# A Fourier mix and sliding-window attention kernel: x's second block loaded early, ring rows, pads and column tiles made by other engines, splits on GpSimd until the masks begin, and a re-ordered tail

## The chip, the core and the metric

The kernel runs on one core of a Trainium2 chip. The metric is the device time of one execution in microseconds (us). Matrix products run on TensorE (PE), elementwise work on VectorE (DVE), ScalarE (ACT) and GpSimd (POOL); SyncE (SP) issues nearly all DMA transfers, in the order of its queue.

## The reference

x has 2048 rows of 512. Two branches are computed from it and mixed row by row with a sigmoid gate:

```
g = sigmoid((x * gate_w).sum(-1))
a, b = x @ dft_hid_re.T, x @ dft_hid_im.T
A = dft_seq_re @ a - dft_seq_im @ b              # Fourier mix, real part
q, k, v = split(x @ wqkv)                        # 32 heads of 16
p = softmax(mask(q k^T / 4))                     # causal, window of 256 keys
B = (p v) @ wo
out = g * A + (1 - g) * B
```

Everything is float32. The kernel splits each float32 operand of the large products into a high part in fp32r and a low remainder, and multiplies three of the four combinations (`TERMS`).

## The kernel before, in words

TensorE's order is written out by the program. One loop over steps n, with four pairs p in each, issues the scores of step n (`s_pair`, L363), the transposed scores of step k = n - 19 (`t_pair`, L445), every few steps the products with v (`pv`, L471), and between them matmuls drawn by `fill` from a generator, `dense`, which holds all other matrix work: v and qk projections (L300 "dv", L277 "dqk"), the hidden transforms ("dab"), and the sequence transform in blocks of 48 matmuls ("dc", L523). The other engines' orders are laid out by a scheduler, with some instructions pinned behind a marked one (`behind`, `mark`, `late`).

What the change touches:

- **Start.** x comes as four blocks of 512 rows, each 512 x 512 values in two loads (`load_x`, L127). Block 0 goes into "pt" buffers, the later ones into the two "raw" buffers, which hold wv first. `split_x` (L133) makes the high part (L78 on ScalarE, L80 on VectorE) and the low part (L81, VectorE). Block 1's casts are made by ScalarE, those of blocks 2 and 3 by VectorE, all as jobs that run between the v projections.
- **Weights.** `split_soon` (L105) queues a cast and a subtraction for each half of a 128 x 1024 weight; `job` runs one of them at every third of six matmuls. All are on VectorE, at the line of `late` (L579).
- **Rings and pads.** "ring" holds q and k in a layout of 128 rows, of which rows 96 to 128 are cleared by GpSimd (L199). A pad (`make_pad`, L333) is the stationary operand of a score; its rows 96 to 128 are set once, for the first kind by GpSimd from x's first low part (L203), for the second by GpSimd memsets and VectorE products (L211, L214). The column tiles "half", "side" and "mrow" are made by GpSimd selects.
- **Evictions.** A qk or ab product is split from PSUM by ScalarE and VectorE into one of three "home" tiles (L84, L86, L88) and stored by SP.
- **Row sums.** Every eight steps `ml_split` (VectorE), `ml_turn` (two small matmuls, L383) and `ml_rows` (VectorE) bring row maxima and sums into the other layout, at places given by `TURN`.
- **v.** `v_load` brings v rows ("vr", one buffer); `v_spread` (L428, GpSimd) spreads them into "vpad". From step 19 on GpSimd also masks the transposed scores (L450, L454).
- **Tail.** After the loop `attention_done` loads and splits wo into the space of ring0. For each block of 128 rows (token block), `wo_prep` loads o and splits it, and `wo_block` multiplies it with wo (12 matmuls, L793) and adds the result to what the other branch left (L795). Between the last dc blocks these are issued in two batches of 96 matmuls.

Of the kernel before, what the change touches and what calls it, by code (L numbers as in the profile page):

```python
# [14 lines left out]
P = 128  # L15
# [17 lines left out]
def fnet_window_mix(ctx: ExitStack, tc: tile.TileContext, xT, x, wqk, wv, wr, wi, cr, ci, wo, gw, out):  # L33
# [40 lines left out]


    def split(hi, lo, raw, act=False):
        if act:
            nc.scalar.copy(hi, raw)  # L78
        else:
            nc.vector.tensor_copy(hi, raw)  # L80
        nc.vector.tensor_sub(lo, raw, f(hi))  # L81

# [44 lines left out]
    def load_x(ss, j):  # L127
        raw = st.tile([P, 1024], F32, name="raw", bufs=2)
        ld(raw.rearrange("p (k s) -> p k s", k=2), xT[ss, 2 * j:2 * j + 2].rearrange("k p s -> p k s"))
        for c in range(2):  # L130
            XRAW[2 * j + c, ss] = raw[:, HALVES[c]]

    def split_x(ss, dks, act=False):  # L133
        for dk in dks:
            XT[dk, ss] = big.tile([P, 2, 512], F32R, name="big")
            split(XT[dk, ss][:, 0], XT[dk, ss][:, 1], XRAW.pop((dk, ss)), act)

# [30 lines left out]
    for h in (0, 64):  # L168
# [6 lines left out]
    nc.gpsimd.memset(f(ident[:]), 1.0)  # L175
    nc.gpsimd.affine_select(ident[:], f(ident[:]), pattern=[[1, P]], compare_op=OP.is_equal, fill=0.0,
                            base=0, channel_multiplier=-1)

    cols = const.tile([P, 4], F32, name="half")
    half, side = cols[:, :2], cols[:, 2:]  # L180
    mrow = const.tile([P, 2], F32, name="mrow")
    for t, edges in ((half, ((0, 16, 32, 48, 64, 80), (16, 32, 48, 64, 80, 96))), (mrow, ((96, 98), (98, 100)))):
        nc.gpsimd.memset(t, 0.0)
        for h in range(2):
            for i, e in enumerate(edges[h]):
                a = t[:, h:h + 1]
                nc.gpsimd.affine_select(a, a, pattern=[[0, 1]], compare_op=OP.is_ge, fill=1.0 - i % 2,
                                        base=e - 1, channel_multiplier=-1)

    nc.vector.reduce_sum(side[:, 0:1], f(ident[:]).rearrange("p (r h) -> p h r", h=2)[:, 0],  # L190
                         axis=mybir.AxisListType.X)
    nc.vector.tensor_scalar(side[:, 1:2], side[:, 0:1], -1.0, 1.0, op0=OP.mult, op1=OP.add)

# [3 lines left out]
    def clear_rows(i, ss):  # L197
        with behind("pool"):
            nc.gpsimd.memset(f(ring[i][96:128, :, ss * 512:(ss + 1) * 512]), 0.0)  # L199

    first_lo = f(XT[0, 0][96:128, 1]).rearrange("r (p c) -> r p c", p=NP)
    for t in pads[0]:
        mark("pool", nc.gpsimd.affine_select(t[96:128], first_lo, pattern=[[0, NP], [0, P]], compare_op=OP.is_gt,  # L203
                                             fill=0.0, base=0, channel_multiplier=0))
    clear_rows(1, 0)
    clear_rows(0, 0)
    vpad = [const.tile([P, 4, NP, 32], F32, name=f"vpad{b}") for b in range(2)]

    def clear_pads():
        for t in pads[1]:  # L210
            nc.gpsimd.memset(f(t[96:128]), 1.0)  # L211
            for h in range(2):
                a = turned(t)[96:128, :, :, h]
                nc.vector.tensor_scalar(a, f(a), mrow[96:128, h:h + 1], None, op0=OP.mult)  # L214


# [117 lines left out]
    def make_pad(i, n):  # L334
# [3 lines left out]
        b = n % NB  # L338
        with behind(*(("act", "dve") if n < NPAD else ())):
            for h in range(2):  # L340
                src = f(ring[i][:96, :, b * BQ:(b + 1) * BQ])
                dst = turned(t)[:96, :, :, h] if i else t[:96, :, 64 * h:64 * h + 64]
                if i and h:
                    nc.scalar.activation(dst, src, AF.Copy, scale=half[:96, h:h + 1])  # L344
                else:
                    nc.vector.tensor_scalar(dst, src, half[:96, h:h + 1], None, op0=OP.mult)  # L346
# [190 lines left out]

    def c_final(get, ab, r):
        ps = ps_d.tile([P, 512], F32, name="dc", tag="d")
        g = g1[:, 15:16]  # L540
        for j in range(2):
            w = get((1, 30 + j))
            yield from c_part(w, range(16)[8 * j:8 * j + 8 - 2 * j], ab, ps, (0, 13))
            yield
        late(nc.vector.scalar_tensor_tensor, r, ps, g, r, OP.mult, OP.add)
        for c, dma in ((slice(0, 256), nc.sync), (slice(256, 512), nc.scalar)):
# [39 lines left out]
    def dense():  # L586
        warm()
        with behind("sp"):
            wraw = [load_raw(wv[i]) for i in range(2)]
        wvs = [late(split_raw, r, True) for r in wraw]  # L590
        qk_first(wq0)
        load_x(1, 0)
        load_x(1, 1)
        yield
        def x_job(ss, dk):
            late(split_x, ss, (dk,), ss == 1)
            if dk % 2 and ss < 3:
                load_x(ss + 1, dk // 2)

# [121 lines left out]
        ab = nxt  # L721
        wait = []

        mixed = {}

# [19 lines left out]
        for tb in range(SWITCH, 16):  # L745
            if FIN:
                while ended:
                    ended.pop(0)()
            if tb in O:
                mixed[tb] = wo_block(tb, 0)  # L750
            for w in [w for w in wait if w in O]:
                wait.remove(w)
                ld(out[w], wo_block(w, 1))
            if FIN and tb < 15:
                for w in (tb + 1, *wait[:-(-len(wait) // (15 - tb))]):
                    wo_prep(w)
            yield from c_block(pieces.get, 1, tb, ab, add_r) if tb < 15 else c_final(pieces.get, ab, mixed.pop(15))

    FIN = []

    def attention_done():
# [70 lines left out]
    ring_ahead(0)  # L832
    need(("v", 5))

# [9 lines left out]
    for n in range(N + LAG + 1):  # L844
        if n in (1, 3, 5):
            for i in range(2):
                clear_rows(1 - i, (n + 1) // 2)
        if n == 7:
            clear_pads()
        k = n - LAG  # L850
        ring_ahead(n + 1)
        if k in (-1, 4):
# [5 lines left out]
        for p in range(NP):  # L858
# [9 lines left out]
            fill(n)  # L868
            for at_n, at_p, do in TURN:
                u, j = divmod(n - at_n, 8)  # L870
# [64 lines left out]
```

## Time and profile before

| | us |
|---|---|
| runs before | 852.27, 853.18, 858.51 (median 853.18) |
| the profiled execution's own time | 854.57 |
| its span, from the first to the last instruction | 852.9 |
| TensorE busy | 844.8 |
| VectorE busy | 615.8 |
| ScalarE busy | 593.7 |
| GpSimd busy | 251.9 |

The profile is of one execution on hardware. A line of a group names the source line, engine, operation, output and inputs, count, busy time and mean duration. A timeline row gives start, duration, engine, line, operation, and in brackets the idle time before it and what ended it. PEld is TensorE's weight load, SPq SyncE's queue.

### The profile page before, as it was taken

Reading aid. Unit: us, or ns where it says so; the run is one execution under the profiler, and the core shown is the slowest. Engines: PE = TensorE matmul, PEld = TensorE weight load, DVE = VectorE, ACT = ScalarE, POOL = GpSimd, SP = SyncE. Lnnn points to the kernel's source line nnn. Section 1 sums busy time; section 2 is a strip of 40 time slices with the busy share of each in tenths; the row PEclk is TensorE's granted clock in tenths of the full one; section 3 lists DMA queues with packets and bytes.
Section 4 is the critical chain, followed back from the end, with each engine's and each line's share of the span. In section 5 each row is a group of like instructions: output and inputs, shape, how many; then the busy total and the mean of one; then the engine's idle time right before and its main releaser. Section 6 shows DMA issues by size and latency. Waiting matters only on the chain.

```text
span 852.9 us, 16687 instructions
## 1 busy us (share of the span) xinstructions
PE 844.8 (99%) x5166; PEld 691.3 (81%) x5166; DVE 615.8 (72%) x2013; ACT 593.7 (70%) x1793; POOL 251.9 (30%) x585
## 2 busy tenths in 40 slices
PE   9999999999999999999999999999999999999998
PEld 7788788788788888888878887888888887877887
DVE  5588978667878787669777787788888774437531
ACT  5388798878888987779878897778777765532200
POOL 9000222333332333333423324333243354510000
PEclk9999999999999999999999999999999999999999
DMA  7876578576675275444435557989784344359542
GB/s 255 276 235 201 172 247 249 198 236 210 205 249 181 59 210 127 152 125 143 148 120 145 164 144 216 286 278 292 242 225 140 117 153 144 124 176 303 158 147 98
DMA packets 94344, 160.99 MB, mean 189 GB/s; under 512 B 26800, under 2 KB 35760, under 8 KB 94256
## 3 DMA queue, kind: packets, MB, share of 16 engines
q1 hardware_dynamic: 93824, 159.28, 59.8%
q8 instruction: 40, 0.66, 0.3%
q10 hardware_dynamic: 432, 0.66, 0.2%
q14 instruction: 48, 0.39, 0.1%
HBM read 108.27 MB, written 51.64 MB: 187 GB/s over the span
## 4 chain that ended last, share of the span: by engine, by line
PE 92%; DMA 4%; DVE 2%; ACT 1%; issue 1%; SPq 0%; DVEq 0%; ACTq 0%
PE dc L523 39%; PE dab L300 10%; PE s L363 9%; PE t L445 8%; PE o L471 8%; PE dqk L277 8%; PE t L793 5%; PE dv L300 4%; DMA raw<-xT 1%; DMA fin<-o_scr 1%; DMA o_scr<-ev 1%; DVE sm L365 1%; DMA pt<-wqk 0%; DVE big L81 0%; SPq L56 0%
## 5 line engine op out<-in xcount | busy, mean ns | idle before, releaser
L368 ACT ACTIVATE sm<-sm,ml 128x320 f32<-128x320 f32 (+4 forms) x512 | 277.9, 544 | 101.1 <-DVE ml L365 96.4
L523 PE MATMUL dc<-big,hi 128*128 128x512 f32 x1020 | 344.4, 393 | 0.0
L365 DVE CUSTOM_DVE_ANT_0 sm<-s,mask 128x320 f32<-128x320 f32 (+4 forms) x512 | 235.3, 464 | 113.2 <-PE s L363 91.5
L523 PE MATMUL dc<-big,lo 128*128 128x512 f32 x510 | 200.6, 393 | 0.0
L523 PEld LDWEIGHTS dc<-big,hi 128*128 128x128 f32 x1020 | 179.7, 188 | 21.4
L446 ACT ACTIVATE pt<-t 128x320 f32<-128x320 f32 (+4 forms) x392 | 160.3, 411 | 43.0 <-PE t L445 40.9
L450 POOL TENSOR_SCALAR_AFFINE_SELECT pt<-pt 128x128 f32<-128x128 f32 x196 | 72.2, 368 | 302.0 <-ACT pt L446 299.8
L363 PE MATMUL s<-ring,pad 128*128 128x320 f32 (+4 forms) x512 | 157.7, 308 | 0.0
L445 PE MATMUL t<-ring,pad 128*128 128x320 f32 (+4 forms) x512 | 154.1, 301 | 0.1
L346 DVE TENSOR_SCALAR pad<-ring,half 96x256 fp32r<-96x256 f32 x384 | 119.9, 358 | 13.5 <-PE t L445 13.3
L363 PEld LDWEIGHTS s<-ring,pad 128*128 128x128 f32 x512 | 96.1, 188 | 30.3 <-issue 9.0
L445 PEld LDWEIGHTS t<-ring,pad 128*128 128x128 f32 x512 | 96.1, 188 | 22.0 <-DVE ml L365 1.0
L523 PEld LDWEIGHTS dc<-big,lo 128*128 128x128 f32 x510 | 95.9, 188 | 13.8 <-issue 1.6
L368 ACT ACTIVATION_READ_ACCUMULATOR sm<-sm,ml 128x1 f32 x512 | 97.7, 191 | 0.0
L428 POOL TENSOR_SCALAR vpad<-vr,half 128x256 f32<-128x256 f32 x64 | 60.5, 958 | 124.9 <-DMA vr<-v_scr 75.7
L579 DVE TENSOR_TENSOR lo<-raw,hi 128x512 fp32r<-128x512 f32 x142 | 96.8, 691 | 0.1
L300 PE MATMUL dab<-hi,big 128*128 128x512 f32 x256 | 89.2, 394 | 0.0
L277 PE MATMUL dqk<-big,hi 128*128 128x512 f32 x240 | 85.7, 394 | 1.5 <-DVE big L81 0.9
L579 DVE CAST hi<-raw 128x512 fp32r<-128x512 f32 x142 | 60.1, 432 | 18.7 <-PE dc L523 13.0
L344 ACT ACTIVATE pad<-ring,half 96x256 fp32r<-96x256 f32 x128 | 66.6, 520 | 0.0
L454 POOL TENSOR_SCALAR_AFFINE_SELECT pt<-pt 128x128 f32<-128x128 f32 x172 | 62.0, 361 | 0.1
L446 ACT ACTIVATE home<-t 128x320 f32<-128x320 f32 (+4 forms) x120 | 49.0, 408 | 13.4 <-PE t L445 11.5
(97 smaller groups left out, 915.3 us busy)
## 6 DMA issues: line engine op xcount, KB each, us to landing
qk_scr<-home SPq DMA_DIRECT2D x32, 512.0 KB
ring<-qk_scr SPq DMA_DIRECT2D x32, 512.0 KB
raw<-cr SPq DMA_DIRECT2D x32, 512.0 KB
raw<-ci SPq DMA_DIRECT2D x32, 512.0 KB
r_scr<-ev SPq DMA_DIRECT2D x42, 256.0 KB
ev<-r_scr SPq DMA_DIRECT2D x42, 256.0 KB
ab_scr<-home SPq DMA_DIRECT2D x20, 512.0 KB
big<-ab_scr SPq DMA_DIRECT2D x20, 512.0 KB
```

Of the source, the lines that this page charges most:

```text
L277: nc.tensor.matmul(ps, w[a][:, c:c + 128], XT[dk, ss][:, b], start=n == 0, stop=n == 11)
L300: nc.tensor.matmul(ps, XT[dk, ss][:, a, c * 128:(c + 1) * 128], wh[b], start=n == 0, stop=n == 11)
L346: nc.vector.tensor_scalar(dst, src, half[:96, h:h + 1], None, op0=OP.mult)
L363: nc.tensor.matmul(ps[:, :w], PAD[0, n][:, p], ring[1][:, p, k0:k0 + w], start=True, stop=True)
L365: mark("dve", nc.vector.tensor_tensor_reduce(out=sm[:, :w], in0=ps[:, :w], in1=mask[:, WIN - w:], scale=1.0, scalar=3e38, op0=OP.add, op1= ...
L368: mark("act", nc.scalar.activation(sm[:, :w], sm[:, :w], AF.Exp, bias=nm[:, c], scale=-1.0, accum_out=l[:, c]))
L445: nc.tensor.matmul(ps[:, :w], PAD[1, n][:, p], ring[0][:, p, q0:q0 + w], start=True, stop=True)
L446: nc.scalar.activation(pt[:, p, :w], ps[:, :w], AF.Exp, scale=-1.0)
L450: nc.gpsimd.affine_select(a, a, pattern=[[0, 2], [2, 64]], compare_op=OP.is_ge, fill=0.0, base=1, channel_multiplier=-1)
L471: nc.tensor.matmul(OT[g, sb][32 * p:32 * p + 32, q - sb * 512:e - sb * 512], v2[:, p], pt[:, p, q - q0:e - q0], start=first, stop=kb == 8 ...
L523: nc.tensor.matmul(ps, w[a][:, i % 8 * 128:i % 8 * 128 + 128], ab[SC[i]][:, b], start=i == ends[0] and a + b == 0, stop=i == ends[1] and a ...
L579: return fn(*args)
```

## The change

It does nine things. Block 1 of x goes into "pt" buffers and is loaded right behind wv, and block 2 then goes into "raw" where block 1 went. Ring rows are cleared in one go, behind a select that reads x's first high part instead of two that read its low part. The second pad of the first kind and the pads of the second kind get their rows from ScalarE. The column tiles are made by VectorE reductions of the identity. Block 3's casts are made by GpSimd, its subtractions stay on VectorE. Weight splits are made by GpSimd until `masks` is filled, at step 19. Pads of the first kind are pinned behind VectorE's last marked instruction up to step 24. The first turn of the row sums is issued at (10, 0) and (10, 1) instead of (9, 1) and (9, 2). In the tail a new `tail_step` runs ahead of every 12 dc matmuls: it multiplies up to two token blocks that were prepared more than two ticks ago, and prepares others, at most seven at a time.

```diff
 def split(hi, lo, raw, act=False):
     if act:
         nc.scalar.copy(hi, raw)
     else:
-        nc.vector.tensor_copy(hi, raw)
-    nc.vector.tensor_sub(lo, raw, f(hi))
+        cast = (nc.gpsimd if act is None else nc.vector).tensor_copy(hi, raw)
+        if act is None:
+            mark("pool", cast)
+    return nc.vector.tensor_sub(lo, raw, f(hi))
...
 # split_soon
-    jobs.append(lambda c=c: late(nc.vector.tensor_copy, hi[:, c], raw[:, c]))
-    jobs.append(lambda c=c: late(nc.vector.tensor_sub, lo[:, c], raw[:, c], f(hi[:, c])))
+    jobs.append(lambda c=c: late((nc.vector if masks else nc.gpsimd).tensor_copy, hi[:, c], raw[:, c]))
+    jobs.append(lambda c=c: late((nc.vector if masks else nc.gpsimd).tensor_sub, lo[:, c], raw[:, c], f(hi[:, c])))
...
 # load_x, split_x
-    raw = st.tile([P, 1024], F32, name="raw", bufs=2)
+    raw = pt_raw() if ss == 1 else st.tile([P, 1024], F32, name="raw", bufs=2)
...
+    for t, run in ((half, 16), (side, 1)):
+        nc.vector.reduce_sum(t[:, 0:1], f(ident[:]).rearrange("p (g h x) -> p h g x", h=2, x=run)[:, 0],
+                             axis=mybir.AxisListType.XY)
...
+first_hi = f(XT[0, 0][96:128, 0]).rearrange("r (p c) -> r p c", p=NP)
+mark("pool", nc.gpsimd.affine_select(pads[0][0][96:128], first_hi, ...))
+for ss in range(4):
+    for i in (1, 0):
+        clear_rows(i, ss)
...
 # clear_pads
+    nc.scalar.activation(pads[0][1][96:128].rearrange("r p c -> r (p c)"),
+                         f(XT[0, 0][96:128, 0]), AF.Copy, scale=0.0)
     for t in pads[1]:
-        nc.gpsimd.memset(f(t[96:128]), 1.0)
         for h in range(2):
-            nc.vector.tensor_scalar(a, f(a), mrow[96:128, h:h + 1], None, op0=OP.mult)
+            nc.scalar.activation(turned(t)[96:128, :, :, h], mask[96:128, :256]...,
+                                 AF.Identity, bias=mrow[96:128, h:h + 1], scale=0.0)
...
 # dense
     with behind("sp"):
         wraw = [load_raw(wv[i]) for i in range(2)]
+        load_x(1, 0)
+        load_x(1, 1)
     wvs = [late(split_raw, r, True) for r in wraw]
     qk_first(wq0)
-    load_x(1, 0)
-    load_x(1, 1)
+    load_x(2, 0)
+    load_x(2, 1)
     def x_job(ss, dk):
-        late(split_x, ss, (dk,), ss == 1)
-        if dk % 2 and ss < 3:
-            load_x(ss + 1, dk // 2)
+        late(split_x, ss, (dk,), ss == 1 or (None if ss == 3 else False))
+        if dk % 2 and ss == 2:
+            load_x(3, dk // 2)
...
 # c_part
     for i in chunks:
+        if FIN and i % 4 == 0:
+            tail_step()
...
+def tail_step():
+    t = next(clock)
+    for tb in [tb for tb in O if born[tb] < t - 2][:2]:
+        if tb in wait:
+            wait.remove(tb)
+            ld(out[tb], wo_block(tb, 1))
+        else:
+            mixed[tb] = wo_block(tb, 0)
+    for tb in (*wait[:5], 15, 14, *wait[5:]):
+        if tb not in O and tb not in mixed and len(O) < 7 and (tb > now[-1] or tb in wait):
+            wo_prep(tb)
+            born[tb] = t
...
+FIRST = (8, 1, ml_split), (10, 0, ml_turn), (10, 1, ml_rows), (12, 0, m_ring)
...
+    if k == 0:
+        masks.append(n)
...
-        for at_n, at_p, do in TURN:
+        for at_n, at_p, do in TURN if n > 12 else FIRST:
```

More of the change, by code (lines that the diff above doesn't have):

```diff
@@ L338, in make_pad @@
         b = n % NB
-        with behind(*(("act", "dve") if n < NPAD else ())):
+        with behind(*(("act", "dve") if n < NPAD else ("dve",) if i == 0 and n < 24 else ())):
             for h in range(2):
@@ L745, in dense @@
         for tb in range(SWITCH, 16):
-            if FIN:
+            now.append(tb)
+            if tb == 15:
                 while ended:
                     ended.pop(0)()
-            if tb in O:
-                mixed[tb] = wo_block(tb, 0)
[L751 to L759, printed above, removed]
+            yield from c_block(pieces.get, 1, tb, ab, add_r) if tb < 15 else c_final(pieces.get, ab)
+    FIN = []
+    now = []
+    wait = []
+    mixed = {}
+    born = {}
+    clock = iter(range(99))
+    def tail_step():
[5 more added lines that the diff above has]
+            else:
+                mixed[tb] = wo_block(tb, 0)
+        for tb in (*wait[:5], 15, 14, *wait[5:]):
+            if tb not in O and tb not in mixed and len(O) < 7 and (tb > now[-1] or tb in wait):
+                wo_prep(tb)
+                born[tb] = t
     def attention_done():
```

55 lines of the change are left out of this document (23 added, 32 removed).

## The prediction, made before the changed kernel had run

> **What bounds the kernel now.** I read the page first, then who TensorE waited for, then its timeline around each wait, then the engine named there.
>
> ```profile
> span 852.9 us, 16687 instructions
> PE 844.8 (99%) x5166; PEld 691.3 (81%) x5166; DVE 615.8 (72%) x2013; ACT 593.7 (70%) x1793; POOL 251.9 (30%) x585
> ...
> PEclk9999999999999999999999999999999999999999
> ```
>
> TensorE is busy 99% at an undisturbed clock, and the change neither adds nor takes away a matmul. So nothing can be won except the moments in which TensorE stands still, and these can be listed.
>
> ```profile
> PE dqk L277 <- DVE big L81: 0.9, 1, 0.9
> ...
> PE t L793 <- ACT os L78: 0.6, 1, 0.6
> ```
>
> Columns: total us, times, longest. Three more waits of this kind stand below with their releaser. The ends of matmuls are modelled, so I measure a stall from start to start. The unhindered pace comes from the chain in order of time (start, us, what), the stalls from TensorE's timeline (start, us, ..., idle time before).
>
> ```profile
> 11.46 3.57 DMA raw<-xT
> ...
> 29.52 5.67 PE dv L300 x25
> ...
> 783.33 22.54 PE t L793 x96
> ```
>
> ```profile
> 8.07 0.73 PE L265 MATMUL s<-big,hi 128*128 128x512 f32 x2 [0.37 <-DVE big L81]
> ...
> 24.76 0.39 PE L277 MATMUL dqk<-big,hi 128*128 128x512 f32 x1
> 26.05 0.50 PE L277 MATMUL dqk<-big,hi 128*128 128x512 f32 x1 [0.91 <-DVE big L81]
> ...
> 94.15 0.27 PE L383 MATMUL s<-ident,mlh 128*64 128x128 f32 x1 [0.72 <-DVE mlh L377]
> ...
> 99.92 0.50 PE L277 MATMUL dqk<-big,hi 128*128 128x512 f32 x1 [0.64 <-DVE home L86]
> ...
> 102.93 0.63 PE L277 MATMUL dqk<-big,hi 128*128 128x512 f32 x2
> 103.68 0.41 PE L445 MATMUL t<-ring,pad 128*128 128x320 f32 x1
> ...
> 783.33 6.97 PE L793 MATMUL t<-fin,os 128*128 128x512 f32 x28 [0.59 <-ACT os L78]
> ```
>
> A 512-column matmul starts every 5.67 / 25 = 0.227 us and is shown as 0.39 long; so a shown idle time is about 0.16 short. At 26: 26.05 - 24.76 - 0.23 = 1.06. In the same way 0.37 + 0.16 = 0.53 at 8.07, 0.88 at 94, 0.80 at 99.9 and 0.75 at 783.33; the 96 matmuls behind this last took 22.54 where 96 x 0.227 = 21.8, so 0.75 more. At 103.68 it is 103.68 - 102.93 - 0.45 = 0.30. In all 5.07, that is 0.6% of the run, and the most this change can take, beside some 0.1 us with which the pipeline restarts behind a stall (0.3 to 0.4 in all).
>
> **The change part by part.** *x's second block.* It goes into two pt buffers and is issued right behind wv, before the third block, on the same SP queue.
>
> ```profile
> 6.94 1.07 DVE L81 TENSOR_TENSOR big<-pt,big 128x512 fp32r<-128x512 f32 x1 [1.08 <-ACT big L78]
> ...
> 8.28 0.68 DVE L81 TENSOR_TENSOR big<-pt,big 128x512 fp32r<-128x512 f32 x1
> ...
> 23.73 0.43 DVE L80 CAST big<-raw 128x512 fp32r<-128x512 f32 x1 [4.42 <-DMA raw<-xT]
> ...
> 25.31 0.69 DVE L81 TENSOR_TENSOR big<-raw,big 128x512 fp32r<-128x512 f32 x1
> ```
>
> ```profile
> 17.48 0.59 ACT L311 COPY ev<-dv 128x512 f32<-128x512 f32 x1 [0.80 <-PE dv L300]
> ```
>
> The wait at 26.05 is not for the second block's load. VectorE stands until 23.73 for block three, whose cast is queued ahead of the last subtraction of block two (25.31, ends 26.0). In the changed order the four subtractions of block two stand together, ahead of block three. ScalarE's casts for them come later, since five pad instructions of at most 512 columns follow the copy at 17.48, at most 0.6 each: 3 us, then a cast, a copy and a cast, 1.8. The last cast ends near 22.9 and the last subtraction near 23.6, against 24.8 when TensorE wants it. So 1.06 plus a restart of 0.1 go: **1.15**. If the early load held wv back, TensorE would wait at its first dv matmul instead, at most the 3.57 us that this load took from issue to landing (11.46 to 15.03); but wv is issued ahead of it, and as many bytes stand behind wv as before. Bounds: -2.4 to 1.2; I take the upper end, since the rows name the cast of block three as the releaser's holder and none names wv.
>
> *Ring clearing and pads.* POOL now has one select behind x's first high part instead of two behind the low one; the column tiles become three more reduces on VectorE near 3 us, and two products behind x's splits, some 0.2 us each, far from anything that TensorE wants.
>
> ```profile
> 6.25 1.23 POOL L203 TENSOR_SCALAR_AFFINE_SELECT pad<-big 32x512 fp32r<-32x512 f32 x2
> 7.42 14.09 POOL L199 MEMSET ring<- 32x2048 f32 x8
> ...
> 90.97 1.84 POOL L428 TENSOR_SCALAR vpad<-vr,half 128x256 f32<-128x256 f32 x2 [67.98 <-DMA vr<-v_scr]
> 100.54 2.38 POOL L428 TENSOR_SCALAR vpad<-vr,half 128x256 f32<-128x256 f32 x2 [7.72 <-DMA vr<-v_scr]
> ```
>
> The subtraction at 6.94 took 1.07 while POOL's selects ran (6.25 to 7.48); its twin at 8.28 took 0.68 while POOL only cleared the ring. It is the releaser of the wait at 8.07. With the selects gone from there it should end 0.39 earlier: **0.4**. The remaining select moves to 4.85, beside the first subtraction; its result is wanted at 5.94, and 0.4 later it is still just in time. Bounds: -0.2 to 0.5. The Trainium skill, "SBUF — State Buffer", Who interferes with whom, says that a VectorE instruction with two SBUF inputs contends with a GpSimd instruction that reads SBUF, not with one that only writes; the two rows agree.
>
> *Splits by POOL.* Until the masks begin (step 19, 100.9 us), 4 casts of x's last block and 5 casts with 5 subtractions of weights leave VectorE, and 4 pad products go to ScalarE.
>
> ```profile
> 91.19 0.80 DVE L579 TENSOR_TENSOR lo<-raw,hi 128x512 fp32r<-128x512 f32 x1
> ...
> 92.02 0.48 DVE L365 CUSTOM_DVE_ANT_0 sm<-s,mask 128x320 f32<-128x320 f32 x1
> ...
> 93.88 0.21 DVE L377 TENSOR_TENSOR mlh<-ml,mlh 128x64 fp32r<-128x64 f32 x1
> ...
> 97.21 0.61 DVE L346 TENSOR_SCALAR pad<-ring,half 96x256 fp32r<-96x256 f32 x2
> ...
> 99.18 0.69 DVE L86 TENSOR_TENSOR home<-dqk,home 128x512 fp32r<-128x512 f32 x1
> ...
> 100.60 1.01 DVE L346 TENSOR_SCALAR pad<-ring,half 96x256 fp32r<-96x256 f32 x2
> ```
>
> The waits at 94, 99.9 and 103.7 are all for VectorE late in its own queue: in this stretch its operations follow each other without a gap, and of what stands ahead of the eviction at 99.18, three casts and two subtractions (by the rows above 3 x 0.43 + 2 x 0.69 = 2.7 us) are weight splits that now go to POOL. The eviction was 0.8 late, so it has room. The first transposition's result at 93.88 has 0.43 + 0.80 + 0.43 = 1.6 fewer us ahead of it and was 0.9 late. Here 2.0 us of stalls (0.88 + 0.80 + 0.30) with two restarts should go; I take **1.9**, since VectorE has little slack there. The turn itself is moved only for the first eight steps, at 66.5 us, where TensorE did not wait: nothing.
>
> What POOL needs for a 128x512 cast or subtraction, no row shows. From below: 8 memsets of 2048 columns in 14.09, so 0.44 for 512. The select reads and writes 512 columns in 0.62. From above: vpad's products, 256 columns in 0.92, give 1.85 for a cast, and twice that, 3.7, for two inputs. I take 0.7 and 1.2, near the select, whose plain run of 512 columns is most alike.
>
> ```profile
> 68.70 0.69 PE dv L300 x3
> ...
> 81.94 0.68 PE dqk L277 x3
> ```
>
> By the chain, TensorE leaves the first qk weight, and with it a buffer, near 68.7, where it goes over to dv, and wants the next weight near 81.9. 2 x 0.7 + 2 x 1.2 = 3.8 us split it by 72.5, 11.1 us at the upper price by 79.8. So POOL's idle time hides it at either end; without that cover VectorE would do it, as before.
>
> *The tail.* The wo blocks, formerly two batches of 96 matmuls, come two at a time between 12 dc matmuls, early token blocks first.
>
> ```profile
> 771.21 6.50 DMA o_scr<-ev
> 777.73 4.90 DMA fin<-o_scr
> ```
>
> ```profile
> 773.63 0.62 ACT L78 CAST os<-fin 128x512 fp32r<-128x512 f32 x1 [0.16 <-DMA fin<-o_scr]
> ...
> 782.66 0.62 ACT L78 CAST os<-fin 128x512 fp32r<-128x512 f32 x1 [6.25 <-DMA fin<-o_scr]
> ```
>
> ```profile
> 777.49 0.68 DVE L81 TENSOR_TENSOR fin<-raw,fin 128x512 fp32r<-128x512 f32 x1
> ```
>
> The wait at 783.33 is for the last o_scr block (stored at 771, landed 777.7, loaded back by 782.6). Now the first blocks are token blocks 0 to 3, whose casts ended by 774.3. They begin 24 matmuls (5.4 us) earlier, at 777.4; the last wo weight is subtracted by 778.2 and wanted at 779.2 to 779.7. Token blocks 15 and 14 are wanted at 796 and 802. VectorE's first sum waits behind their subtractions (784.6); with four PSUM buffers TensorE needs that sum only at 793.8. So 0.75 + 0.75 go, less what the interleaving may cost at first: **1.1**; bounds -1.5 (if the last wo weight is 2.6 us late) to 1.5.
>
> **Sum.** 1.15 + 0.4 + 1.9 + 1.1 = 4.55: the profiled execution's span of 852.9 becomes 848.3, and its time of 854.57 becomes 850.0. It lies 1.4 above the median of the runs, 853.18; from the median I forecast **848.6**. With all stalls and restarts gone (5.4) and the runs' lower edge of 852.27 it is 846.9.
>
> **The rivals.** *One: VectorE gains little, since POOL gets in its way.* For it speaks that the two pads at 100.60 took 1.01 beside POOL's vpad and the two at 97.21 took 0.61, and the subtraction at 91.19 0.80 instead of 0.69. If each of ten POOL operations costs VectorE 0.4, 4 of the 5.6 us taken off it (5 x 0.43 + 5 x 0.69) come back, and of the 1.9 about 0.4 stays: 853.18 - (1.15 + 0.4 + 0.4 + 1.1) = 850.1. Against it: the s operation at 92.02, of the kind that fills VectorE, took 0.48 beside vpad, no more than others. The same section of the Trainium skill calls the shared port an exclusive lock held for the whole instruction; by that a clash with a POOL subtraction of 1.2 costs up to 1.2, and rival one would hold.
>
> *Two, slower: SyncE stands behind POOL.* In the changed queue the second vr load, which waits for POOL's vpad, comes ahead of the store of the next qk eviction, and vpad comes behind POOL's weight splits.
>
> ```profile
> 90.27 4.81 SPq L56 DMA_DIRECT2D qk_scr<-home  x2
> ...
> 97.09 0.37 SPq L56 DMA_DIRECT2D vr<-v_scr  x1
> ```
>
> Buffers two and three come free near 81.9, behind the last dv matmul, and three casts and three subtractions follow: at the upper price 81.9 + 3 x 5.55 + 1.84 = 100.4 for vpad, and the store due at 95 goes out 5 us late; the third vr load repeats it with the next (vr lands 3.4 later, vpad takes 2.4: 106.2 instead of 98, an estimate from 95 and a turn of 3.3). Three home tiles at 3.3 us a turn give 10 us; 8 late and 3 to land misses that, ScalarE stands in an eviction with the exponentials behind it, and TensorE follows by some 3 us each time. 6 lost and 1.9 not won: 853.18 - 2.65 + 6 = 856.5. It decides from a cast and a subtraction that take 4.45 together (then vpad ends after 97.1). Against it: the select's 0.62.
>
> *Three: the tail's wait only moves.* A ci load now goes ahead of three o loads, and a ci cast stands between the two last subtractions of wo. If it lands 2.6 us late, the tail loses 1.5 instead of winning 1.1: 851.2.
>
> **How the numbers follow.** Forecast 0.70, rival one 0.13, two 0.10, three 0.05, more than 1% faster 0.02 (no row shows that much idle time). The range reaches from 846.5 to 853.5: it leaves out rival two and the ends. 1% (8.5 us) is about what a measurement of this kernel can tell from no change. Faster by over 1%: 0.02; slower by over 1%: 0.06, the part of rival two where the hold lasts longer than I priced it; within: 0.92.
>
> **What would show it.** Right: none of the five waits above 0.2 in TensorE's list; block two's subtractions ended by 23; POOL's casts below 1 and subtractions below 2; the first wo block without a wait. Wrong: a POOL subtraction above 3.7, SyncE waiting for vpad at 95 to 105, pads above 0.9 for two beside POOL's splits, or TensorE waiting for fin near 777.

## The result, and the profile after

The changed kernel takes **850.38 us** (median, 849.25 to 851.73) beside 853.18 (852.25 to 858.51) of the kernel before: a ratio of **0.9962, 95% interval 0.9947 to 0.9977**. On a second chip it was 849.77 beside 853.12, 0.9968 (0.9955 to 0.9980). The forecast was 848.6, with a range of 846.5 to 853.5: direction, range and "within 1%" hold, and of the 4.55 us that were to be won 2.8 to 3.35 came. All runs counted here were undisturbed, and the ratios weigh every run, so they need not be the quotient of the medians.

The page's first lines, and the whole list of what TensorE waited for (total us, times, longest):

```profile
span 850.0 us, 16674 instructions
...
PE 844.5 (99%) x5166; PEld 691.5 (81%) x5166; DVE 610.7 (72%) x1999; ACT 593.2 (70%) x1798; POOL 258.4 (30%) x578
```

```profile
PE dv L592 <- DVE ev L150: 1.5, 1, 1.5
PE t L448 <- DVE ml L368: 0.5, 1, 0.5
```

The first line is the start of the program, as before. None of the five waits of the prediction is left, and there is a new one. TensorE's timeline at the old places, and at the new one:

```profile
24.42 0.61 PE L280 MATMUL dqk<-big,hi 128*128 128x512 f32 x2
...
92.33 0.54 PE L386 MATMUL s<-ident,mlh 128*64 128x128 f32 x2
...
97.68 0.50 PE L280 MATMUL dqk<-big,hi 128*128 128x512 f32 x1
...
101.08 0.31 PE L448 MATMUL t<-ring,pad 128*128 128x320 f32 x1
...
545.93 0.41 PE L448 MATMUL t<-ring,pad 128*128 128x320 f32 x1 [0.52 <-DVE ml L368]
...
775.41 5.66 PE L811 MATMUL t<-fin,os 128*128 128x512 f32 x24
```

TensorE's order is the same in both kernels until the wo blocks, but for the two small matmuls of the first turn, which moved from 66.5 to behind 69. So the two traces can be laid side by side matmul by matmul: how far a matmul's start in one kernel lies ahead of the same matmul's in the other tells where time is won and lost, to hundredths of a us. The table does this against the first profile of before (time of that profile along the top; the experiments are explained below). At 67 the kernels with the moved turn have its two matmuls still ahead of them; this makes that column 0.17 higher than the time really won (the changed kernel is 1.54 ahead at 60 and at 66.3).

| us ahead of before at | 24 | 27 | 67 | 74 | 92 | 105 | 125 | 540 | 549.5 | 765 | end |
|---|---|---|---|---|---|---|---|---|---|---|---|
| changed kernel | 0.34 | 1.54 | 1.71 | 0.94 | 0.90 | 2.72 | 2.74 | 2.70 | 1.76 | 1.73 | 2.93 |
| the same again (e10) | -0.11 | 1.09 | 1.26 | 0.47 | 0.45 | 2.74 | 2.68 | 3.43 | 3.70 | 3.70 | 4.92 |
| before again (e9) | 0.02 | 0.29 | 0.26 | 0.26 | 0.26 | 0.67 | -0.29 | 0.38 | 0.43 | 0.40 | 0.30 |
| weights by VectorE (e1) | 0.31 | 1.51 | 1.68 | 1.44 | 1.40 | 0.12 | 0.21 | 0.41 | 0.68 | 0.68 | 1.90 |
| first weight by VectorE (e2) | 0.38 | 1.58 | 1.75 | 1.52 | 0.20 | 1.96 | 1.98 | 2.18 | 1.58 | 1.55 | 2.76 |
| only casts by POOL (e3) | 0.20 | 1.39 | 1.57 | 1.34 | 1.34 | 2.67 | 2.73 | 2.94 | 1.72 | 1.72 | 2.94 |
| ab tiles earlier (e4) | 0.44 | 1.63 | 1.81 | 1.04 | 0.86 | 2.66 | 2.66 | 3.41 | 3.68 | 3.68 | 4.90 |
| the same again (e11) | 0.13 | 1.32 | 1.50 | 0.73 | 0.73 | 2.99 | 2.85 | 2.83 | 2.67 | 2.67 | 3.89 |
| x late (e6) | -0.25 | 0.95 | -0.11 | -0.87 | -0.90 | 1.37 | 1.09 | 1.84 | 1.86 | 1.85 | 3.08 |
| tail of before (e7) | -0.06 | 1.14 | 1.31 | 0.53 | 0.51 | 2.61 | 2.63 | 3.35 | 1.88 | 1.85 | 3.07 |
| casts by POOL, ab earlier (e8) | 0.03 | 1.22 | 1.40 | 1.17 | 1.17 | 2.50 | 2.45 | 2.93 | 2.76 | 2.74 | 3.95 |
| tail alone (e12) | 0.02 | -0.02 | -0.05 | -0.05 | -0.05 | 0.37 | -0.91 | -0.71 | -1.49 | -1.48 | -0.26 |

In the first line 1.20 is won at 26, 1.82 between 92 and 105, and 1.20 in the tail, much as forecast. But 0.60 is **lost at 70** (1.71 less the 0.17 of the moved turn, down to 0.94) and 0.94 **at 545**, where nothing had been looked for. The rows at 67 to 71 of VectorE, POOL and ScalarE:

```profile
66.52 1.18 POOL L587 CAST hi<-raw 128x512 fp32r<-128x512 f32 x2 [28.48 <-PE dqk L280]
67.57 1.66 DVE L349 TENSOR_SCALAR pad<-ring,half 96x256 fp32r<-96x256 f32 x2
67.66 2.73 POOL L587 TENSOR_TENSOR lo<-raw,hi 128x512 fp32r<-128x512 f32 x2
...
70.33 0.56 ACT L371 ACTIVATE sm<-sm,ml 128x320 f32<-128x320 f32 x1 [1.66 <-DVE ml L368]
```

The two pads, 0.61 elsewhere, took 1.66 while POOL split the first weight; the masked scores behind them came late, and so the exponentials. At 545 VectorE stood for a load:

```profile
541.92 0.74 DVE L706 SCALAR_TENSOR_TENSOR ev<-dc,g,ev 128x512 f32<-128x512 f32 x1
544.26 0.43 DVE L587 CAST hi<-raw 128x512 fp32r<-128x512 f32 x1 [1.59 <-DMA raw<-cr]
```

POOL's splits cost 0.59 for a cast (1.18 for two) and 1.37 for a subtraction (2.73 for two).

### The profile page after: what moved, and what is told of

It reads as the page before. It is cut to its first block, busy times and chain, and to the rows that moved or that the text cites. A ratio compares the mean times of both kernels' runs of the same rounds, so it can differ in the third digit from the quotient of the medians.

```text
span 850.0 us, 16674 instructions
## 1 busy us (share of the span) xinstructions
PE 844.5 (99%) x5166; PEld 691.5 (81%) x5166; DVE 610.7 (72%) x1999; ACT 593.2 (70%) x1798; POOL 258.4 (30%) x578
## 4 chain that ended last, share of the span: by engine, by line
PE 98%; DVE 1%; DMA 0%; issue 0%; ACT 0%; POOL 0%; DVEq 0%; ACTq 0%
PE dc L528 41%; PE dab L303 10%; PE dqk L280 9%; PE s L366 9%; PE t L448 8%; PE o L474 8%; PE t L811 5%; PE dv L303 5%; PE s L268 1%; DMA raw<-wqk 0%; PE dv L592 0%; DVE pad L349 0%; PE s L386 0%; ACT sm L371 0%; DVE sm L368 0%
## 5 line engine op out<-in xcount | busy, mean ns | idle before, releaser
L349 DVE TENSOR_SCALAR pad<-ring,half 96x256 fp32r<-96x256 f32 x384 | 121.7, 363 | 14.1 <-PE t L448 13.8
L587 DVE TENSOR_TENSOR lo<-raw,hi 128x512 fp32r<-128x512 f32 x137 | 93.3, 690 | 0.1
L587 DVE CAST hi<-raw 128x512 fp32r<-128x512 f32 x137 | 57.8, 431 | 18.8 <-PE dc L528 14.2
```

The source lines that it names most:

```text
L587: return fn(*args)
```

## The experiments

The medians, beside before's on the same chip (before for e1 to e4: 853.77; e6 to e8: 853.47; e9 to e12: 853.12):

| kernel | median us | ratio, 95% interval | span of its profile |
|---|---|---|---|
| e1 weights by VectorE | 854.22 | 0.9997 (0.9979 to 1.0016) | 851.0 |
| e2 first weight by VectorE | 851.64 | 0.9969 (0.9951 to 0.9988) | 850.1 |
| e3 only casts by POOL | 851.85 | 0.9968 (0.9951 to 0.9985) | 850.0 |
| e4 ab tiles earlier | 850.90 | 0.9952 (0.9934 to 0.9970) | 848.0 |
| e6 x late | 852.79 | 1.0001 (0.9988 to 1.0015) | 849.8 |
| e7 tail of before | 851.13 | 0.9968 (0.9952 to 0.9984) | 849.8 |
| e8 casts by POOL, ab earlier | 852.38 | 0.9988 (0.9973 to 1.0003) | 849.0 |
| e9 before again | 854.26 | 1.0008 (0.9997 to 1.0019) | 852.6 |
| e10 changed kernel again | 849.77 | 0.9968 (0.9955 to 0.9980) | 848.0 |
| e11 ab tiles earlier again | 850.73 | 0.9976 (0.9965 to 0.9987) | 849.0 |
| e12 tail alone | 853.85 | 1.0018 (1.0005 to 1.0031) | 853.2 |

The kernel before against itself (e9) differs by 1.1 us in the medians; smaller differences than that are read from the traces here, not from the times. A profile is of one execution: that of e1 is the fastest of its twelve and that of e6 the second fastest, so their spans look better than their ratios.

**e1: weights by VectorE.**

```diff
-            jobs.append(lambda c=c: late((nc.vector if masks else nc.gpsimd).tensor_copy, ...
-            jobs.append(lambda c=c: late((nc.vector if masks else nc.gpsimd).tensor_sub, ...
+            jobs.append(lambda c=c: late(nc.vector.tensor_copy, ...
+            jobs.append(lambda c=c: late(nc.vector.tensor_sub, ...
```

> All weight splits (casts and subtractions of the halves) on VectorE, as before the change; the casts of x's last block stay on POOL. My theory: the win of 1.83 us at 94 to 104 belongs to these splits and so does the loss of 0.69 us at 70 to 72, where two pads took 1.66 us beside a POOL subtraction. So here the two pads at 67 to 68 take about 0.6 us again, TensorE stays 1.66 us ahead at 72, and the waits near 92 to 101 return (about 1.8 us in all). TensorE is then only some 1.7 us ahead at 540, where the changed kernel gave back 0.9 us of its 2.7 to a late load of cr, so almost nothing is given back: the time is that of the changed kernel within 0.3 us (850.2 to 850.8), although 1.1 us less was won early. Rival: the wait at 545 is a fixed piece of this schedule and has nothing to do with how far TensorE is ahead; then the time is 851.4 to 851.8. Second rival, for 70 us: the loss comes from the turn that was moved there, not from POOL; then it stays at 0.69 and the time is 0.7 more still.

Measured: the pads at 67 took 0.61 again, and of the 0.60 lost at 70 0.07 is left (1.68 - 0.17 - 1.44); so **0.53 is POOL's**, and the moved turn, the second rival, costs 0.07 at most. The time missed the expectation: 854.22, no gain at all. At 92 to 105 TensorE does not only lose the 1.82 of the changed kernel but falls back by 1.28 against before:

```profile
93.87 0.27 PE L386 MATMUL s<-ident,mlh 128*64 128x128 f32 x1 [1.85 <-DVE mlh L380]
...
103.95 0.50 PE L280 MATMUL dqk<-big,hi 128*128 128x512 f32 x1 [0.86 <-DVE home L92]
```

Here the wait for the turn is 1.85 where before had 0.72. TensorE came 1.4 earlier, VectorE had the weight splits in its queue again, and at 105 they are where before was (0.12 ahead). In this stretch VectorE sets the time: **what is won ahead of it counts only if its queue is shortened too**. So the splits on POOL are worth 1.82 + 1.28 = 3.1 there, or 2.6 with the clash.

**e2: only the first weight by VectorE.**

```diff
-                w = split_soon(raw)
+                w = split_soon(raw, True)        # casts and subtractions on VectorE
```

> Only the first weight (second group of qk, at 66 to 70 us) is split by VectorE; the later ones stay on POOL. My theory: the port clash at 70 us goes (pads 0.6 us for two, TensorE 1.66 us ahead at 72 instead of 0.97), the win of 1.8 at 94 to 104 stays, so TensorE is 3.4 us ahead at 110. If what is won is given back at 545 (a load at the pace of the DMA queues), TensorE is no more than about 2 us ahead at 548 and the time is 850.2 to 850.6, as the changed kernel's. Rival, the wait at 545 is a fixed 0.9: the whole 0.7 stays, 849.7. Rival, the loss at 70 is not POOL's: TensorE 0.97 ahead at 72 and the time unchanged, with pads at 1.66 still.

Measured: no clash at 67 (1.52 ahead at 74), but the clash came back at 84, where three POOL subtractions now stood beside the next two pads:

```profile
84.29 2.77 DVE L349 TENSOR_SCALAR pad<-ring,half 96x256 fp32r<-96x256 f32 x2
84.32 3.87 POOL L587 TENSOR_TENSOR lo<-raw,hi 128x512 fp32r<-128x512 f32 x3
...
87.72 0.50 PE L280 MATMUL dqk<-big,hi 128*128 128x512 f32 x1 [1.06 <-DVE home L92]
```

2.77 for two pads instead of 0.61, about two POOL subtractions of 1.29 each. That settles that POOL's subtractions hold the pads up, wherever the two meet, and it cost more here (1.32 from 74 to 92) than it had saved (0.58 at 74). So the lead of 3.4 at 110 that I expected was 1.96 at 105.

**e3: POOL casts, VectorE subtracts.**

```diff
-            jobs.append(lambda c=c: late((nc.vector if masks else nc.gpsimd).tensor_sub, ...
+            jobs.append(lambda c=c: late(nc.vector.tensor_sub, ...
```

> POOL makes the casts of the weights (one input), VectorE the subtractions (two inputs). My theory: it is the POOL subtraction, which reads two tiles, that holds VectorE's pads up, so the two pads near 68 us take 0.6 to 0.7 us and TensorE is 1.6 us ahead at 72. VectorE has two subtractions (1.4 us) of the 2.7 us taken off it back ahead of the eviction at 97 to 99, so about half of the 1.8 won there stays: 2.5 us ahead at 104. Rival, any POOL instruction that reads SBUF holds VectorE: pads 1 us or more beside the casts, 0.97 ahead at 72. The time is 850.2 to 850.8 by either, since the wait at 545 gives back what is won above some 1.8.

Measured: pads at 0.61, 1.34 ahead at 74 and 2.67 at 105, as much as the changed kernel's 2.72 with the subtractions on POOL. The casts alone are enough for the stretch at 92; moving the subtractions bought nothing that the clash did not take back. The pads stood only 0.1 beside the casts here, so this run does not tell whether casts hold them; e5 does.

**e5: the clash by itself.**

```python
for v in ("pad", "cast", "sub", "psub"):             # VectorE: six of one kind
    for g in ("none", "memset", "select", "vpad", "cast", "sub"):  # POOL: three of one kind
        nc.scalar.activation(ga, a, AF.Copy, scale=1.0)            # both read ga
```

> The disputed cost by itself; the kernel computes nothing of the reference. In each of 24 rounds VectorE runs six instructions of one kind (pad: tensor_scalar 96x256; cast: 128x512; sub: 128x512 with two SBUF inputs; psub: 128x512 with one SBUF and one PSUM input) while GpSimd runs nothing, memsets, selects, vpad's product in eight pieces of 32, casts or subtractions of 128x512, three each. Both start when ScalarE has written their common input. My theory (pads stood still for whole POOL subtractions of 1.3 us): a pad or a cast of VectorE beside a POOL subtraction takes up to 1.3 us and ends with it, instead of 0.34 and 0.42; beside POOL casts up to 0.6; beside memsets and alone nothing is added; a subtraction with one PSUM input is never held. Rival (bandwidth is shared, no lock): each takes some part longer, 1.2 to 1.6 times, and POOL's ends later too. What two SBUF inputs do beside POOL is open: in the kernels before and after, the subtractions of 128x512 beside vpad took 0.00 to 0.12 more.

The groups by line (busy us, mean ns; tile names say VectorE's kind and POOL's):

```profile
L66 DVE TENSOR_SCALAR v_pad_none<-ga,col 96x256 fp32r<-96x256 f32 x6 | 2.1, 349 | 4.4 <-ACT ga L48 4.2
L66 DVE TENSOR_SCALAR v_pad_memset<-ga,col 96x256 fp32r<-96x256 f32 x6 | 3.0, 498 | 0.9 <-ACT ga L48 0.8
L66 DVE TENSOR_SCALAR v_pad_vpad<-ga,col 96x256 fp32r<-96x256 f32 x6 | 2.7, 449 | 1.0 <-ACT ga L48 0.8
L66 DVE TENSOR_SCALAR v_pad_cast<-ga,col 96x256 fp32r<-96x256 f32 x6 | 3.1, 519 | 1.2 <-ACT ga L48 1.0
L66 DVE TENSOR_SCALAR v_pad_sub<-ga,col 96x256 fp32r<-96x256 f32 x6 | 4.9, 816 | 1.0 <-ACT ga L48 0.8
L68 DVE CAST v_cast_none<-ga 128x512 fp32r<-128x512 f32 x6 | 2.6, 427 | 0.9 <-ACT ga L48 0.8
L68 DVE CAST v_cast_memset<-ga 128x512 fp32r<-128x512 f32 x6 | 3.5, 579 | 0.9 <-ACT ga L48 0.8
L68 DVE CAST v_cast_sub<-ga 128x512 fp32r<-128x512 f32 x6 | 5.4, 898 | 0.9 <-ACT ga L48 0.8
L70 DVE TENSOR_TENSOR v_sub_none<-ga,other 128x512 fp32r<-128x512 f32 x6 | 4.1, 692 | 0.9 <-ACT ga L48 0.8
L70 DVE TENSOR_TENSOR v_sub_memset<-ga,other 128x512 fp32r<-128x512 f32 x6 | 4.2, 704 | 0.9 <-ACT ga L48 0.8
L70 DVE TENSOR_TENSOR v_sub_sub<-ga,other 128x512 fp32r<-128x512 f32 x6 | 7.0, 1162 | 0.9 <-ACT ga L48 0.8
L72 DVE TENSOR_TENSOR v_psub_none<-ga,ps 128x512 fp32r<-128x512 f32 x6 | 4.1, 687 | 0.9 <-ACT ga L48 0.8
L72 DVE TENSOR_TENSOR v_psub_sub<-ga,ps 128x512 fp32r<-128x512 f32 x6 | 4.1, 686 | 1.0 <-ACT ga L48 0.8
...
L63 POOL TENSOR_TENSOR g_sub_sub<-ga,other 128x512 fp32r<-128x512 f32 x3 | 4.9, 1647 | 3.0 <-ACT ga L48 2.8
L63 POOL TENSOR_TENSOR g_psub_sub<-ga,other 128x512 fp32r<-128x512 f32 x3 | 3.8, 1268 | 3.3 <-ACT ga L48 3.1
```

The single pads beside POOL's subtractions:

```profile
L66 DVE TENSOR_SCALAR v_pad_sub<-ga,col x6: 349/793/1305, 23.2 to 27.9; 96x256 fp32r<-96x256 f32 x6
```

Shortest, median, longest. Three of the six pads are plain (0.349 to 0.350) and three are held (1.236 to 1.305); each held one ends 0.15 behind a POOL subtraction. Six pads lost 6 x (0.816 - 0.349) = 2.8 us to three subtractions. For POOL's subtractions the theory of a lock holds and the rival of shared bandwidth falls. It does not hold for every POOL instruction: beside POOL's product in eight pieces a pad took 0.449 on the mean, and one that started behind the product ended 0.31 before it, so it was slowed and did not wait for the end.

The other rows say whom it hits: VectorE's casts and two-input subtractions as much as the pads (0.47 more each on the mean), an instruction with a PSUM input not at all (686 to 687 beside everything). Beside memsets, which only write, the two-input subtractions are hardly held (0.704), but the pads (0.498) and casts (0.579) are, which I had not expected; the first POOL instruction of these rounds is a cast of 256 columns, but three pads and three casts that stood beside memsets alone took 0.57 and 0.71 as well.

The Trainium skill, "SBUF — State Buffer", Who interferes with whom, says this in advance: VectorE's casts and tensor_scalar in their two-port mode, and its instructions with two SBUF inputs against POOL's reads, share a port pair with GpSimd, and the loser waits for the whole instruction. By that rule the prediction's rival one had its mechanism. The rows of POOL's subtractions and memsets agree with it; that of its product in pieces (0.449, a slowing and no wait for the whole instruction) does not.

**e4: two ab tiles earlier.** The second half's ab tiles are loaded between 516 and 560; two of these loads go out one step earlier in SyncE's order.

```diff
-            if next(calls) * 8 % (2 * SWITCH) >= 8:
+            if (n := next(calls)) % 3 == (2 if n < 6 else 1):
```

> The changed kernel; only two loads of the second half's ab tiles (256 KB hi and 256 KB lo each) are issued one step earlier in SyncE's order, ahead of other loads, between 516 and 540 us. No engine's order changes but SyncE's. My theory: the load of cr that came late at 544 waits on the queue for the ab tile that was issued ahead of it; with that tile 3 to 7 us earlier the load goes out near 537.2, when its buffer is free, and lands by 541 to 542; the wait of 0.9 at 545 goes and the time is 849.3 to 849.6. Rival: the 16 DMA engines are busy all the time from 520 to 560 (share 0.97 to 1.02), so no order helps; the wait stays or another load is late by as much, 850.2 to 850.6.

Measured: no wait at 545 and a span of 848.0, 2.0 less. That looked like a version that beats the changed kernel; e10 and e11 do not bear it out.

**e6: x late.**

```diff
-        raw = pt_raw() if ss == 1 else st.tile([P, 1024], F32, name="raw", bufs=2)
+        raw = st.tile([P, 1024], F32, name="raw", bufs=2)
...
-            load_x(1, 0)
-            load_x(1, 1)
         wvs = [late(split_raw, r, True) for r in wraw]
         qk_first(wq0)
-        load_x(2, 0)
-        load_x(2, 1)
+        load_x(1, 0)
+        load_x(1, 1)
...
-            if dk % 2 and ss == 2:
-                load_x(3, dk // 2)
+            if dk % 2 and ss < 3:
+                load_x(ss + 1, dk // 2)
```

> The changed kernel, only x's second block loaded where it was before, into raw buffers behind the first block's, with the third block's load issued block by block. In this kernel VectorE's order still has the four subtractions of block two ahead of block three's first cast, so it tells the load apart from the order. My theory, as in the prediction: the wait of 0.91 at 26.05 was for VectorE standing at block three's cast, not for the load of block two; with this order it stays away without the early load too: TensorE 1.2 to 1.5 us ahead at 27 and the time within 0.3 of the changed kernel. Rival: the load was late; then the wait returns, TensorE is 0.3 ahead at 27 and, with the give-back at 545, the time is 0.3 to 1.2 longer.

Measured: at 27 the 1.2 is won without the early load, so the wait at 26 belonged to VectorE's order, as the prediction had it. But by 60 all of it is lost:

```profile
32.40 0.43 DVE L82 CAST big<-raw 128x512 fp32r<-128x512 f32 x1 [2.47 <-DMA raw<-xT]
...
34.53 0.60 DVE L349 TENSOR_SCALAR pad<-ring,half 96x256 fp32r<-96x256 f32 x2
...
35.23 0.27 PE L366 MATMUL s<-ring,pad 128*128 128x64 f32 x1 [1.00 <-issue]
```

Block three's second half lands late, its two casts and subtractions stand ahead of the first pads, and the first scores start 1.23 late (the releaser is not named; the pads end at 35.1). The early load is worth its 1.2 at 35, not at 26. The runs of this kernel gain nothing (1.0001), so the second half of my theory, a time within 0.3 of the changed kernel's, falls.

**e7: the tail of before**, in the changed kernel.

```diff
-            if FIN and i % 4 == 0:
-                tail_step()
...
+            if FIN and tb < 15:
+                for w in (tb + 1, *wait[:-(-len(wait) // (15 - tb))]):
+                    wo_prep(w)
```

> The changed kernel with the tail of before (wo blocks in two batches of 96 matmuls). My theory: until 770 us nothing differs (TensorE 1.8 us ahead of before at 550 to 770), the wait for the last o_scr block returns at 781 to 782 with about 0.6 shown, and the 96 matmuls take 22.5 us again: the span is 851.1, 1.1 longer than the changed kernel's. Rival: the tail gained nothing of its own and the end is as early without it, 850.0.

Measured: a span of 849.8, and no wait at the first wo block. My theory falls here; the rival is right. From 765 to the end it wins 1.22, the same as with the new tail.

```profile
779.47 0.62 ACT L80 CAST os<-fin 128x512 fp32r<-128x512 f32 x1 [6.24 <-DMA fin<-o_scr]
```

```profile
780.72 19.62 PE L798 MATMUL t<-fin,os 128*128 128x512 f32 x85
```

The last o_scr block is cast 3.2 earlier than before (782.66), TensorE arrives 1.9 earlier, and the cast is in time. Why the block came 1.3 earlier than the lead explains is open, and this is one execution.

**e8: casts by POOL, and the ab tiles earlier** (e3 and e4 together).

> POOL makes the weights' casts, VectorE their subtractions (no clash with the pads), and the two ab tiles are loaded one step earlier. My theory: 2.6 us ahead at 104 as with the casts alone, no wait at 545, the tail 1.1 to 1.2 more: a span of 848.0 to 849.0. Rival: the early ab tiles helped only by the phase of that one run, and the wait at 545 returns with 0.9: 849.9.

Measured: a span of 849.0, no clash, no wait of TensorE at 545, as expected; the median, 852.38, is no better than the changed kernel's. Its ratio, 0.9988, is not even clearly below 1, though e3 and e4 alone had 0.9968 and 0.9952; why is open.

**e9 to e12: before, the changed kernel, and e4 once more, and before with the new tail alone.** e9 and e10 have no edit, e11 has that of e4, e12 has the lines of e7 the other way round in the kernel before. They tell what is the kernel's and what one execution's.

> The kernel before once more, unchanged, for a second profile of it: the prediction took every stall from one execution, whose time was 1.4 above the median of the runs. My theory now: the waits that end in VectorE's own queue (26.05, 94, 99.9, 103.7) stand in every execution with the same length within 0.2; those that end in a load (8.07, 783.33) are partly that execution's own, since with the tail of before put back the wait at 783 stayed away. So the wait at 783 is here below 0.3, and the span 851.5 to 852.5. Rival: all five waits are there as in the first profile, and the span is 852.9 within 0.4.

> The changed kernel once more, for a second profile. My theory: the loss at 70 to 72 (pads held by a POOL subtraction) is in the order of the instructions and returns with 0.5 to 0.7; the wait at 545 for the load of cr returns if TensorE gets there more than 1.8 us ahead of the first profile of before, which it does (2.7), so it loses 0.7 to 1.2 again: span 849.0 to 850.0. Rival: the wait at 545 belongs to that execution alone (the first profile was the longest of eleven runs); then it is not here, and the span is 848.5 to 849.0.

> The changed kernel with the two ab tiles loaded one step earlier, again beside the changed kernel on the same chip. If the wait at 545 is in every execution of the changed kernel, this one is 0.7 to 1.2 us faster than it in the medians; if it belongs to single executions, the two medians are within 0.3. In its profile the load of cr is again there before VectorE wants it at 542.

> The kernel before with the changed kernel's tail and nothing else of the change. By the prediction the tail wins 1.1 of itself: 0.9987 of before's time. By the rival, to which the run with the tail of before points (the wait at 783 had gone without the change), it wins 0 to 0.3: 0.9997 to 1.0000. In the profile nothing differs from before until 770 us but by chance, and no wait stands ahead of the first wo block.

What TensorE waited for in the second profile of before:

```profile
PE dv L584 <- DVE ev L146: 1.5, 1, 1.5
PE s L383 <- DVE mlh L377: 0.7, 1, 0.7
PE t L793 <- ACT os L78: 0.7, 1, 0.7
PE dqk L277 <- DVE home L86: 0.7, 1, 0.7
PE dqk L277 <- DVE big L81: 0.6, 1, 0.6
PE dab L300 <- DVE home L88: 0.5, 1, 0.5
PE s L265 <- DVE big L81: 0.3, 1, 0.3
```

The first line is again the start of the program. The five waits are there again, the tail's too (0.7): I had expected that one to be chance, and it stands in both profiles. The waits for VectorE's queue are less constant than I expected (within 0.2): that at 26 is 0.27 shorter, and between 92 and 105 0.41 less is lost. Another wait, for home at L88, is new: 0.73 lost between 112 and 125, in e12 as well (1.12), in neither profile of the changed kernel, and not in e1 either. The second profile of the changed kernel has only the wait at the program's start:

```profile
PE dv L592 <- DVE ev L150: 1.5, 1, 1.5
```

The clash at 70 is the same (two pads 1.66, 1.26 - 0.17 - 0.47 = 0.62 lost), the wait at 545 is **not** there. And e11 is no faster than e10 (850.73 and 849.77). So the wait at 545 is not in every execution, and moving the ab tiles buys nothing that the medians show. My idea that TensorE's lead is given back there falls as a rule: e10 came 3.43 ahead and lost nothing, e12 came 0.71 *behind* before and lost 0.78. VectorE stood 0.61 and 0.45 for the load in the two profiles of before, 1.59 and not at all in the two of the changed kernel.

Still, the wait is no rarity: in five profiles with the changed kernel's order of loads (the first, e2, e3, e6, e7) VectorE stood until 544.1 to 544.4, whatever TensorE's lead, and four of them lost 0.60 to 1.47 there. With the ab tiles earlier VectorE stood until 543.2 (e8, e11) or not at all (e4), and at most 0.17 was lost; e11 thus missed the expectation that the load is there by 542. Why a queue that is busy all that time (the DMA engines' share is 0.92 to 1.03 from 520 to 560 in the profiles of before and of the changed kernel) differs so between executions stays open.

e12 wins 1.22 in its tail like all others, yet its median is 0.7 above before and its ratio, 1.0018, lies outside both forecasts for it. The losses at 112 to 125 and at 545 in its profile explain the span (853.2), not why they should be commoner with this tail; that stays open.

## Why the prediction was right or wrong

**(a) x's second block, 1.15: right in size and place.** 1.20 in the first pair of profiles, 0.93 in the second (the wait was shorter in e9); block two's last subtraction ended at 22.35, against 23.6 foreseen, ahead of block three's cast:

```profile
21.66 0.69 DVE L85 TENSOR_TENSOR big<-pt,big 128x512 fp32r<-128x512 f32 x1 [0.31 <-ACT big L80]
22.27 0.42 DVE L82 CAST big<-raw 128x512 fp32r<-128x512 f32 x1
```

The reason was half right: VectorE's order cured the wait at 26, and without the early load the stall would have appeared at 35 (e6). That second stall was in no step.

**(b) The selects, 0.4: right on VectorE, not steady on TensorE.** The subtraction at 7.01 took 0.69, not 1.07, and in the first profile TensorE is 0.32 ahead behind it. In the second x landed 0.5 later (VectorE's first cast at 4.82, not 4.32) and TensorE was 0.11 behind. Over the nine profiles with this start (all rows but e9, e12 and e6) the column at 24 reaches from -0.11 to 0.44: the 0.34 of the first profile is in part luck, since x's landing was taken as fixed. The price moved to another instruction, as the step said, and was hidden:

```profile
4.88 1.09 POOL L202 TENSOR_SCALAR_AFFINE_SELECT pad<-big 32x512 fp32r<-32x512 f32 x1 [1.29 <-DVE big L82]
...
5.39 0.86 DVE L163 TENSOR_TENSOR lo<-pt,hi 128x256 fp32r<-128x256 f32 x1
7.01 0.69 DVE L85 TENSOR_TENSOR big<-pt,big 128x512 fp32r<-128x512 f32 x1 [0.76 <-ACT big L80]
...
```

**(c) Splits by POOL, 1.9: right at 94 to 104 (1.82, and 2.29 - 0.41 = 1.88 in the second pair), wrong at 66 to 70.** POOL's prices were 0.59 and 1.37 (taken: 0.7 and 1.2). The step that failed is "POOL's idle time hides it at either end": it looked at when the weight was wanted, and not at which VectorE instruction stood beside the subtraction. The sign named for this, pads above 0.9 for two beside POOL's splits, came twice: 1.66 at 67, and at 88

```profile
88.20 1.39 DVE L349 TENSOR_SCALAR pad<-ring,half 96x256 fp32r<-96x256 f32 x2
```

Rival one had priced the clash at 0.4 for each of ten POOL operations, 4 in all; it was 1.05 and 0.78 for two pairs of pads. The first cost TensorE 0.53, the second nothing that can be seen (0.94 ahead at 74, 0.90 at 92); otherwise the subtractions at 80 and 87 ran beside scores read from PSUM. In the second profile the two pairs took 1.66 and 0.95. Rival one was right in its mechanism and too dear in its price. The step also undercounted: without the splits, (a) would have been lost again at 94 (e1).

**(d) The tail, 1.1: right in size, but the new tail is not needed for it.** 1.20 in the first profile and 1.22 in the second, and the new tail alone wins 1.22 in its profile (e12). But with the old tail the changed kernel has it as well (e7), in its profile and in its runs (0.9968, where the changed kernel has 0.9962 and 0.9968). So in the changed kernel this term cannot be put down to the new tail, and no run's time shows a gain by the new tail alone. That the wait at 783 goes whenever the rest is earlier is likely from e7, but one profile does not show it.

**The sum.** The first two profiles differ by 2.9, the second two by 4.6, the medians by 2.8 and 3.35. Against the 4.55 the first pair lacks the clash (0.53), the 0.07 beside it, and the load at 545 (0.94), and these make 1.54 (4.55 - 1.54 = 3.01, beside 2.93 measured). That the second pair comes to 4.6, as the sum had it, is partly luck: it has the clash too (0.62), and the new wait of before (0.73), which was in no term, makes up for it. The forecast's step from a profile to the median treated every stall of one execution as the kernel's; the load at 545 shows that some are not, and the new wait of before that a profile can also miss one. Rival two did not happen: the second vr load went out at 91.65 and the store after it at 93.84, since a cast and a subtraction took 1.96 together, far below 4.45. Rival three's wait did not come either.

## What to carry to other kernels

A job given to an idle engine is priced twice: by when its result is wanted, and by what the first engine runs at that moment; here two pads of 0.61 together took 0.95 to 2.77 beside POOL's subtractions, and VectorE's subtractions with an operand in PSUM lost nothing beside them (0.69). Terms that wait for the same engine's queue do not add: take each part away from the changed kernel, not only one by one from the old. Before a stall that ends in a load is put into a sum, look for it in a second execution.

## What the runs showed of the hardware that was not expected

- A VectorE pad of 0.349 us took up to 1.305 beside POOL subtractions of 1.27 (e5); in e2 two pads took 2.77 beside POOL subtractions of 1.29. Beside them single pads took 0.35 or 1.24 to 1.31 in e5, nothing between; beside POOL's product in pieces they were only slowed (0.449 on the mean).
- Both lose: beside VectorE's two-input subtractions POOL's own took 1.65 on the mean instead of 1.27, and VectorE's two-input subtractions 1.16 instead of 0.69 (e5). A POOL select of 128x128 beside them took 0.71 instead of 0.29, at no cost to VectorE (0.69).
- POOL casts 128x512 from fp32 to fp32r in 0.59 to 0.61 us and subtracts the same in 1.27 to 1.37, near the 0.7 and 1.2 taken from the select.
- The same kernel's same load, in a stretch where the DMA engines are busy throughout (share 0.92 to 1.03), came from 0 to 1.59 us after VectorE was ready for it.
